# An order by hand, operation by operation, for the first stage of a memory-attention and bilinear-FFN kernel, and half of w3 w_out in three fp32r products

## The chip, the cores and the metric

The kernel runs on one core of a Trainium2 chip. The metric is the time of one execution on the device in microseconds (us), the median of the runs shown. In the text PE is the matrix engine, PEld its loading of weights, DVE the vector engine, ACT the scalar engine, SP the engine that starts the loads and stores; "granted clock" is the share of full speed that the profile records for PE.

## The reference

For each of 8 sequences (576 tokens, 8 heads of 64) an attention over 32 memories per head, then a bilinear feed-forward layer over all 4608 tokens. The weights come to the device as fp64, q, k, v and phi as fp32.

```python
a = softmax(phi, over the 32 memories)             # b h s m
k_m = einsum('bhsm,bhsd->bhmd', a, k)              # memories of keys and values
v_m = einsum('bhsm,bhsd->bhmd', a, v)
attn = softmax(q @ k_m.T / 8)                      # b h s m
x = (attn @ v_m).transpose(0, 2, 1, 3).reshape(4608, 512)
h = (x @ w1) * (x @ w2) @ w3                       # w1, w2: 512x1024, w3: 1024x1024
return h @ w_out                                   # w_out: 1024x512
```

## The kernel before

The kernel folds weights together. w3 w_out (1024x512) is made once and called W; for each sequence, v_m times w1 and w2 gives small "memory weights" (256 rows), so that x @ w1 is the softmaxed scores times them. Large products over tokens are fp32r matmuls in three parts: each operand is split into a high part (rounded to fp32r, a cast on ACT) and a low part (what is left, a subtraction on DVE, `split`, L117), and high*high, low*high and high*low are added in psum. Products that are made once, as w3 w_out, are plain fp32 matmuls.

The steps and their names in the order tables:

- Loads and conversions. `TILES` (L23 to L26) lists the weights' 26 pieces: 14 of w3's first half and w_out in turn (0 to 13), four pairs of w3's second half, w31 (14 to 17), eight of w1 and w2, w12 (18 to 25; two for each of four column groups q). They come as fp64, 512 KB for pieces 0 to 11 and 1 MB for the others. `convert` (C, L348) makes fp32 of a piece: two ACT operations on the high and low words (L370, L373), a shift on DVE (L375) and an addition on DVE (L376). `fetch` starts the loads into seven buffers, the last four pieces into the buffers of kv and q (L340).
- `product(r, k)` (W, L380): one of eight k steps of half r of w3 w_out, 4 matmuls 128x512 each (L386), into psum banks a, b, a, b (r = 0) or o, o, a, b (r = 1). `keep(r, i)` (K, L394) splits a finished bank into Wh, Wl.
- The attention of a sequence: `top`, `exp`, `norm` (softmax of phi), `turn` (transposes on PE, L187 and L191), `mem` (the memories, L202 and L211), `blocks` (transposes, L227, and km, vm on DVE), `sc` (scores, L242, and transposes on DVE, L251), `se`, `sn` (softmax), `pr` (transpose and split into ah, al).
- `N` (L295): memory weights of a column group q: 8 matmuls L301, and a split into mh, ml.
- `ab_unit` (A, L435): one of 16 units of a sequence: 12 fp32r matmuls (L447) into a and b, a copy of a on ACT, the product on DVE (gr), and its split into gh, gl.
- `out_part` (O, L463): a quarter of a 128-token block's out: 6 fp32r matmuls L471 on gh, gl, Wh, Wl.

The order: PE's and SP's instructions always stand in program order. For the first stage, `START` (L28) and the beginning of `FIRST` up to its first O, ACT's and DVE's order is given too (`by_hand`, L406), step by step: a step's instructions follow each other on each engine. After that a scheduler places ACT's and DVE's work. Sequence 0 has its 16 A units with the tail of W in between, its O parts are mixed with the attention of sequence 1, and so on (`SECOND`, `STEADY`).

## Time and profile before

| | us |
|---|---|
| median of 3 runs | 551.26 |
| lowest run, highest run | 550.85, 670.66 |
| the profiled execution | 549.36 |
| its span in the profile | 547.4 |

| engine | busy us | share of the span |
|---|---|---|
| PE | 529.7 | 97% |
| PEld | 428.1 | 78% |
| DVE | 303.5 | 55% |
| ACT | 246.0 | 45% |

Times in the profile count from the start of the span. A line of the timeline reads: start, length, engine, source line, operation, out<-in, shapes, count, and in brackets the idle time before it and what ended it. A line of the waits reads: who waited, for whom, us in total, times, longest. By the timeline the first half of w3 w_out runs from 7.8 to 37.8 us, the memories of sequence 0 follow, its second half runs from 43.3 to 73.0 us with N0 within it, the A units of sequence 0 from 74.0 to 107.1 us, its first O matmul starts at 111.39 us.

### The profile page before, as it was taken

Reading aid. Unit: us, or ns where it says so; the run is one execution under the profiler, and the core shown is the slowest. Engines: PE = TensorE matmul, PEld = TensorE weight load, DVE = VectorE, ACT = ScalarE, POOL = GpSimd, SP = SyncE. Lnnn points to the kernel's source line nnn. Section 1 sums busy time; section 2 is a strip of 40 time slices with the busy share of each in tenths; the row PEclk is TensorE's granted clock in tenths of the full one; section 3 lists DMA queues with packets and bytes.
Section 4 is the critical chain, followed back from the end, with each engine's and each line's share of the span. In section 5 each row is a group of like instructions: output and inputs, shape, how many; then the busy total and the mean of one; then the engine's idle time right before and its main releaser. Section 6 shows DMA issues by size and latency. Waiting matters only on the chain.

```text
span 547.4 us, 9722 instructions
## 1 busy us (share of the span) xinstructions
PE 529.7 (97%) x4024; PEld 428.1 (78%) x4024; DVE 303.5 (55%) x586; ACT 246.0 (45%) x502; POOL 0.7 (0%) x6
## 2 busy tenths in 40 slices
PE   4999989989999999999999999999999999999997
PEld 1443458966998689968996799869986899689985
DVE  5658886567366715593458425673567045915400
ACT  7766764635454425452544325443544044514310
POOL 0000000000000000000000000000000000000000
PEclk9999989999999999999999999999999999999999
DMA  8999436036334410072007210441021100010011
GB/s 343 420 418 418 172 114 256 1 113 230 111 147 169 173 41 21 1 279 83 20 1 281 81 40 1 155 176 50 2 74 53 40 20 2 20 45 15 1 38 57
DMA packets 14939, 64.05 MB, mean 117 GB/s; under 512 B 1712, under 2 KB 1968, under 8 KB 10032
## 3 DMA queue, kind: packets, MB, share of 16 engines
q1 hardware_dynamic: 14896, 63.45, 30.3%
q8 instruction: 31, 0.51, 0.4%
q14 instruction: 12, 0.10, 0.1%
HBM read 54.00 MB, written 9.44 MB: 116 GB/s over the span
## 4 chain that ended last, share of the span: by engine, by line
PE 91%; DVE 4%; ACT 4%; DMA 1%; issue 0%; SPq 0%; DVEq 0%; ACTq 0%
PE o L471 37%; PE a L447 19%; PE b L447 19%; PE a L386 3%; PE b L386 3%; PE a L301 2%; PE o L202 2%; PE x L301 2%; DVE w L376 1%; PE x L187 1%; PE b L301 1%; ACT w L370 1%; ACT u L373 1%; PE x L202 1%; DMA raw<-in_weights 1%; PE x L242 1%
## 5 line engine op out<-in xcount | busy, mean ns | idle before, releaser
L471 PE MATMUL o<-Wh,gh 128*128 128x512 f32 x288 | 115.1, 400 | 2.0 <-DVE Wl L119 2.0
L471 PE MATMUL o<-Wl,gh 128*128 128x512 f32 x288 | 112.9, 392 | 0.0
L471 PE MATMUL o<-Wh,gl 128*128 128x512 f32 x288 | 112.7, 391 | 0.0
L458 DVE TENSOR_TENSOR gr<-b,a_sb 128x288 f32<-128x288 f32 x128 | 58.5, 457 | 85.6 <-PE b L447 82.8
L118 ACT CAST gh<-gr 128x288 fp32r<-128x288 f32 x128 | 55.4, 433 | 103.8 <-DVE gr L458 103.8
L119 DVE TENSOR_TENSOR gl<-gr,gh 128x288 fp32r<-128x288 f32 x128 | 58.7, 459 | 63.0 <-ACT gh L118 62.9
L447 PE MATMUL a<-ah,mh 128*128 128x288 f32 x256 | 77.8, 304 | 2.2 <-ACT a_sb L456 2.2
L447 PE MATMUL a<-ah,ml 128*128 128x288 f32 x256 | 76.4, 298 | 0.0
L447 PE MATMUL b<-ah,mh 128*128 128x288 f32 x256 | 76.1, 297 | 0.0
L447 PE MATMUL b<-ah,ml 128*128 128x288 f32 x256 | 76.1, 297 | 0.0
L447 PE MATMUL a<-al,mh 128*128 128x288 f32 x256 | 75.2, 294 | 0.0
L447 PE MATMUL b<-al,mh 128*128 128x288 f32 x256 | 75.1, 293 | 0.0
L471 PEld LDWEIGHTS o<-Wh,gh 128*128 128x128 f32 x288 | 54.1, 188 | 24.8 <-issue 11.7
L489 ACT COPY osb<-o 128x512 f32<-128x512 f32 x31 | 18.1, 585 | 101.8 <-PE o L471 88.7
L471 PEld LDWEIGHTS o<-Wl,gh 128*128 128x128 f32 x288 | 54.1, 188 | 12.1
L471 PEld LDWEIGHTS o<-Wh,gl 128*128 128x128 f32 x288 | 54.2, 188 | 10.9
L447 PEld LDWEIGHTS a<-ah,mh 128*128 128x128 f32 x256 | 48.5, 189 | 5.4 <-ACT a_sb L456 2.5
L456 ACT COPY a_sb<-a 128x288 f32<-128x288 f32 x128 | 50.3, 394 | 2.0 <-PE a L447 1.7
L447 PEld LDWEIGHTS a<-al,mh 128*128 128x128 f32 x256 | 49.1, 192 | 0.3
L447 PEld LDWEIGHTS b<-al,mh 128*128 128x128 f32 x256 | 49.2, 192 | 0.0
L447 PEld LDWEIGHTS b<-ah,mh 128*128 128x128 f32 x256 | 48.6, 190 | 0.0
L447 PEld LDWEIGHTS b<-ah,ml 128*128 128x128 f32 x256 | 48.4, 189 | 0.0
(90 smaller groups left out, 633.3 us busy)
## 6 DMA issues: line engine op xcount, KB each, us to landing
kv<-in_kv SPq DMA_DIRECT2D x16, 1024.0 KB, 7.1
raw<-in_weights SPq DMA_DIRECT2D x10, 1024.0 KB, 19.4
q<-in_qT SPq DMA_DIRECT2D x8, 1152.0 KB, 10.4
out<-osb SPq DMA_DIRECT2D x31, 256.0 KB, 2.0
raw<-in_weights SPq DMA_DIRECT2D x12, 512.0 KB, 8.2
ph<-in_phiT SPq DMA_DIRECT2D x8, 576.0 KB, 3.9
kv<-in_weights SPq DMA_DIRECT2D x3, 1024.0 KB, 17.6
kv<-in_kv SPq DMA_DIRECT2D x8, 256.0 KB, 7.9
```

Source lines behind the costliest of these rows:

```text
L118: nc.scalar.copy(out=hi, in_=src)
L119: engine.tensor_tensor(out=lo, in0=src, in1=hi.bitcast(F32), op=ALU.subtract)
L187: nc.tensor.transpose(ps[:, c, t], v["ph"][:, t, at : at + P], ident)
L202: nc.tensor.matmul(ps[t][h * M : (h + 1) * M, : 2 * D], lhsT=v["a"][:, i, t, h * M : (h + 1) * M], rhs=kvt[i][:, (4 * t + h) * 2 * D : (4 ...
L242: nc.tensor.matmul(ps[t][g * M : (g + 1) * M], lhsT=km[b % 2][t * D : (t + 1) * D, g], rhs=v["q"][t * D : (t + 1) * D, g, n * HALF : (n + ...
L301: nc.tensor.matmul(ps[t][g * M : (g + 1) * M], lhsT=vm[b % 2][d, g], rhs=w12_sb[q][d, :, g], start=True, stop=True,)
L386: nc.tensor.matmul(pw[r][i], lhsT=x[:, i * P : (i + 1) * P], rhs=wos[k // half][:, k % half], start=k == 0, stop=k == NF - 1,)
L447: nc.tensor.matmul(p, lhsT=x[:, t, w, fc : fc + P], rhs=y[:, n, t * HALF : (t + 1) * HALF], start=i == 0, stop=i == len(todo) - 1,)
L456: nc.scalar.copy(out=a_sb, in_=ps[0])
L458: nc.vector.tensor_tensor(out=gr, in0=ps[1], in1=a_sb, op=ALU.mult)
L471: nc.tensor.matmul(v["p"], lhsT=x[f][:, at : at + P], rhs=y[f // half][:, f % half], start=f == 0 and k == 0, stop=f == NF - 1 and k == 2,)
L489: nc.scalar.copy(out=osb, in_=v["p"])
```

## The change

Up to the first O, the order is now a list of single operations, `START`, each word of which issues one instruction or a small group: steps are generators that stop (`yield`) after each, and a name that comes again goes on with its step. So `C5 W01 C5 C5 exp.0` puts a matmul group between the operations of one conversion. L names a load, C a conversion, W a product (one bank at a time), K a split of W, G and H a split of an operand. What stood in `FIRST` up to the first O is in `START` now, and nearly all of it stands elsewhere than before: conversions interleave with the softmax, `exp.0` is taken apart, A units overlap. The last piece's second ACT operation, as an instance, comes among the A units.

The second half of w3 w_out (r = 1) is made of high and low parts: `hi_lo` splits the four pairs of w_out (G0 to G3) and of w31 (H0 to H3), each by a cast on ACT and a subtraction on DVE of 128x1024, and `product` issues three fp32r matmuls in place of one fp32 matmul: 96 for 32. The new parts lie in buffers that are free at that time: w_out's high parts in that of w12's last column group and of al, the low parts in ah's, in w_out's own, in those of the memory weights. So w12's last group is converted late (C24, C25), after its place is free. Tags of some buffers change with that (`m_tags`, four small `wo` tiles for two large ones, W's second half in them). Loads: phi goes ahead of pieces 5 and 6, pieces 16 and 17 ahead of q.

Three places of the order. The first, on PE: the end of the memories of sequence 0 (x is the attention's psum, L202 and L211 the memories, L227 the transposes, L242 the scores, L386 the product's second half). Before:

```order
L202 MATMUL x<-kv_190,a 32x128 x8
L211 MATMUL x<-kv_192,a 32x128 x8
L227 MATMUL x<-ident,kvm 128x128 x2
L242 MATMUL x<-q,km_77 32x288 x8
L386 MATMUL o<-wo_87,w_255 128x512 x2
L386 MATMUL a<-wo_87,w_255 128x512
L386 MATMUL b<-wo_87,w_255 128x512
```

And now, where L463 is the product and woh, ah, m_299 are high and low parts of w_out and w31:

```order
L228 MATMUL x<-kv_208,a 32x128 x8
L237 MATMUL x<-kv_213,a 32x128 x8
L463 MATMUL o<-woh,m_299 128x512
L463 MATMUL o<-woh,ah 128x512
L463 MATMUL o<-ah,m_299 128x512
L463 MATMUL o<-woh,m_299 128x512
L463 MATMUL o<-woh,ah 128x512
L463 MATMUL o<-ah,m_299 128x512
L254 MATMUL x<-ident,kvm 128x128 x2
```

The transposes come after two banks of the product's first step, and the scores (not shown) 21 product matmuls later.

The second, on DVE: after km and vm of sequence 0 are there, while PE makes the product's second half. Before:

```order
L251 STREAM_TRANSPOSE s_sb<-x 128x288 x2
L258 TENSOR_REDUCE st_364<-s_sb 128x18
L259 TENSOR_TENSOR s_sb<-s_sb,st_364 128x576
L265 TENSOR_REDUCE ss_368<-s_sb 128x18
L266 TENSOR_SCALAR ss_368<-ss_368 128x18
L267 RECIPROCAL ss_368<-ss_368 128x18
L268 TENSOR_TENSOR s_sb<-s_sb,ss_368 128x576
L375 TENSOR_SCALAR w_381<-w_381 128x1024
L376 ISA w_381<-w_381,u 128x2048
```

And now, from the conversion of the last w31 pair (w_402) on:

```order
L417 ISA w_402<-w_402,u 128x2048
L447 TENSOR_TENSOR m_433<-w_374,m_417 128x1024
L447 TENSOR_TENSOR m_440<-w_402,m_435 128x1024
L280 STREAM_TRANSPOSE s_sb<-x 128x288 x2
L415 TENSOR_SCALAR w_0_81<-w_0_81 128x1024
L417 ISA w_0_81<-w_0_81,u 128x2048
L280 STREAM_TRANSPOSE s_sb<-x 128x288 x2
L287 TENSOR_REDUCE st_483<-s_sb 128x18
L289 TENSOR_TENSOR s_sb<-s_sb,st_483 128x576
```

The softmax of the scores stands behind the subtractions for w31 (L447) and among conversions of w12 (w_0 is its first column group).

The third, on PE: the memories of sequence 1. Before:

```order
L202 MATMUL x<-kv_615,a 32x128 x8
L211 MATMUL x<-kv_617,a 32x128 x8
L471 MATMUL o<-Wh_85,gh_518 128x512
L471 MATMUL o<-Wh_85,gl_526 128x512
L471 MATMUL o<-Wl_86,gh_518 128x512
```

And now:

```order
L540 MATMUL a<-ah,ml_912 128x288
L228 MATMUL x<-kv_784,a 32x128 x8
L228 MATMUL x<-kv_795,a 32x128 x8
L228 MATMUL x<-kv_784,a 32x128 x8
L228 MATMUL x<-kv_795,a 32x128 x8
L237 MATMUL x<-kv_800,a 32x128 x8
L540 MATMUL b<-ah,mh_911 128x288
```

They stood directly before the first O; they stand now within the thirteenth of the 16 A units (L540).

The diff, cut to its core (of START three lines):

```diff
 START = """
-phi0 C C C C C C C W00 C W01 C kv0 q0 top C exp W02 norm C W03 W04 C C turn4 C C W05 C turn0 W06 W07 K03 K01 K02 K00 mem blocks sc0 se0 sn0 W10 C C
-sc1 W11 C C se1 pr0 sn1 W12 W13 C C W14 C N C C C W15 W16 pr1 W17 K12
+L0 L1 L2 L3 L4 phi0 L5 C0 L6 C0 C0 L7 C0 C1 C1 C1 L8 C1 W00 W00 C2 C2 C2 W00 L9 C2 C3 C3 C3 W00 L10 C3 C4 C4 C4 W01 G0
...
+W06 C15 L21 C14 W06 C15 C15 W07 H0 C15 W07 G3 W07 H0 K01 W07 K02 K01 H1 mem.0 K02 G3 K03 K00 K03 W10 L22 mem.0 H1 L23
+C16 W10 blocks.0 K00 W10 C16 C16 W10 blocks.0 W11 C17 C16 W11 C17 W11 C17 W11 H2 C17 W12 sc1.0 H2 H3 W12 H3 W12 C18
...
 FIRST = """
-K13 N phi1 A A A kv1 A top N q1 A A A A A A N exp norm A A turn4 A A turn0 A A mem K10 K11
 O O blocks O sc0 sc1p Mp se0 q2 sn0 O O kv2 pr0 O O O se1 sn1 O Mp Mp M O pr1 O phi2 O O O O O
...
-    def split(hi, lo, src, engine=nc.vector):
+    def split(hi, lo, src):
         nc.scalar.copy(out=hi, in_=src)
-        engine.tensor_tensor(out=lo, in0=src, in1=hi.bitcast(F32), op=ALU.subtract)
+        yield
+        nc.vector.tensor_tensor(out=lo, in0=src, in1=hi.bitcast(F32), op=ALU.subtract)
...
-    m_tags = (2, 3, 4, 0, 5, 6, 7, 1)
+    m_tags = (1, 7, 2, 0, 3, 5, 4, 6)
...
-    wos = [const.tile([P, half, DO], F32, name=f"wo{i}", tag=f"wo{i}") for i in range(2)]
+    wos = [const.tile([P, 2, DO], F32, name=f"wo{i}", tag=f"wo{i}") for i in range(half)]
...
+    def hi_lo(what, k):
+        x = (wos if what == "G" else w31s)[k]
+        if what == "H":
+            hi = spare(const, f"m{k + 1}", 2 * DO)
+        elif k < 2:
+            if k == 0:
+                room = const.tile([P, 4, DO], F32R, name="woh", tag=f"w12_{NQ - 1}")
+                his["G", 1] = room[:, 2:]
+                hi = room[:, :2]
+            else:
+                hi = his["G", 1]
+        else:
+            hi = spare(att, "al", NT * S, bufs=2)
+        his[what, k] = hi
+        nc.scalar.copy(out=hi, in_=x)
+        yield
+        if k == 0:
+            lo = spare(att, "ah", NT * S, bufs=2)
+        else:
+            lo = spare(const, f"wo{k - 1}" if what == "G" else f"m{(0, 5, 6)[k - 1]}", 2 * DO)
+        los[what, k] = lo
+        nc.vector.tensor_tensor(out=lo, in0=x, in1=hi.bitcast(F32), op=ALU.subtract)
+
     def product(r, k):
...
-        x = w3s.pop((r, k))
+        x, y = w3s[r, k], wos[k // 2][:, k % 2]
+        pairs = [(x, y)]
+        if r == 1:
+            (xh, yh), (xl, yl) = [[z[what, k // 2][:, k % 2] for what in "HG"] for z in (his, los)]
+            pairs = [(xh, yh), (xl, yh), (xh, yl)]
         for i in range(4):
-            nc.tensor.matmul(
...
+            for j, (x, y) in enumerate(pairs):
+                nc.tensor.matmul(
+                    pw[r][i],
+                    lhsT=x[:, i * P : (i + 1) * P],
+                    rhs=y,
+                    start=k == 0 and j == 0,
+                    stop=k == NF - 1 and j == len(pairs) - 1,
+                )
+            yield
...
+    def go_on(what):
+        if what not in under_way:
+            under_way[what] = begin(what)
+        next(under_way[what], None)
```

## Prediction

> **What bounds the kernel now.** I read the page first, then PE's own waits, then a table by stage.

> ```profile
> span 547.4 us, 9722 instructions
> PE 529.7 (97%) x4024; PEld 428.1 (78%) x4024; DVE 303.5 (55%) x586; ACT 246.0 (45%) x502; POOL 0.7 (0%) x6
> PE 91%; DVE 4%; ACT 4%; DMA 1%; issue 0%; SPq 0%; DVEq 0%; ACTq 0%
> ```

> PE is busy 97% of the span, and 91% of the chain that ended last is PE. So the time falls only by less PE work or by shorter pauses of PE. The waits of PE, in total:

> ```profile
> PE a L386 <- DVE wo L376: 7.8, 1, 7.8
> PE a L447 <- ACT a_sb L456: 2.2, 1, 2.2
> PE o L471 <- DVE Wl L119: 2.0, 1, 2.0
> PE x L242 <- issue: 1.2, 1, 1.2
> PE x L227 <- ACT kvm L220: 0.8, 1, 0.8
> ```

> The first, 7.8 us, is the first weight on its way in; the change leaves it. The other four, 6.2 us, all lie in the first 111 us. The windows show where, and what the other engines do there (columns: window, its length, busy us of PE, PEld, DVE, ACT, POOL, granted clock, DMA share, GB/s):

> ```profile
> 7.80:37.80 30.00, 30.00 (x73) 13.54 (x73) 20.11 (x31) 22.75 (x33) 0.00 (x0) 1.00 1.02 419
> 37.80:43.30 5.50, 3.48 (x100) 2.30 (x99) 3.55 (x8) 2.68 (x6) 0.00 (x0) 1.00 1.02 419
> 43.30:74.00 30.70, 30.70 (x119) 12.46 (x112) 27.46 (x38) 24.22 (x25) 0.00 (x0) 1.00 0.65 262
> 74.00:85.60 11.60, 9.38 (x72) 8.14 (x64) 8.49 (x14) 5.30 (x12) 0.00 (x0) 0.85 0.49 184
> 96.30:111.40 15.10, 13.12 (x170) 12.43 (x162) 8.01 (x18) 9.72 (x24) 0.00 (x0) 1.00 0.01 2
> ```

> From 7.8 to 37.8 (first half of w3 w_out) PE never pauses; from 43.3 to 74 (second half) neither does it, while DVE is busy 27.46 of 30.7 us. From 74 to 85.6 there is a pause and a clock of 0.85. After 111.4 the order is the old one; I take that part over unchanged.

> **Term 1, the products.** Second half of w3 w_out: 32 fp32 matmuls go, 96 fp32r ones come. Four fp32 products, and 24 steps of an fp32r matmul of the same 128x512 shape with weights of its own each time:

> ```profile
> 51.11 1.88 PE L386 MATMUL o<-wo,w 128*128 128x512 f32 x4
> 54.54 1.88 PE L386 MATMUL o<-wo,w 128*128 128x512 f32 x4
> ...
> 118.30 0.39 PE L471 MATMUL o<-Wh,gl 128*128 128x512 f32 x1
> ...
> 123.79 0.39 PE L471 MATMUL o<-Wh,gl 128*128 128x512 f32 x1
> ```

> From 51.11 to 54.54 four products start: 3.43/4 = 0.858 us each, 27.5 us for 32. From 118.30 to 123.79 there are 24 matmuls: 5.49/24 = 0.229 us each, 22.0 us for 96. Term 1 is -5.5 us. The same shape and the same loading of weights leave little doubt here.

> **Term 2, the clock.** One stretch runs at half clock:

> ```profile
> 79.00:82.20 3.20, 3.20 (x15) 3.20 (x14) 2.20 (x5) 1.16 (x3) 0.00 (x0) 0.50 0.70 208
> 78.11 0.40 PE L447 MATMUL a<-ah,mh 128*128 128x288 f32 x1 [2.22 <-ACT a_sb L456]
> 81.01 0.44 PE L447 MATMUL a<-ah,ml 128*128 128x288 f32 x1
> 81.25 0.44 PE L447 MATMUL a<-ah,mh 128*128 128x288 f32 x1
> 87.32 0.30 PE L447 MATMUL a<-ah,mh 128*128 128x288 f32 x1
> 88.90 0.30 PE L447 MATMUL a<-ah,mh 128*128 128x288 f32 x1
> ```

> It follows the longest pause, 2.22 us. A unit of 12 matmuls takes 88.90 - 87.32 = 1.58 us, 0.132 each; in the half-clock stretch the steps are 0.24. Some 14 matmuls at 0.11 more are 1.5 us. If the change leaves no pause of that length, this goes: -1.5 us. The two other pauses, 2.0 us in all at 41 to 42.6 and 2.0 at 109 to 111, brought no slow stretch; so it may go either way near 2 us, and below 1.3 us I expect none. [...]

> **Term 3, the pauses.** First the ones that go. The 0.79 and 1.23 us stand where PE went from the memories to the transposes to the scores, each waiting for ACT or DVE to bring over what the last one made (the first place shown above). Now six product matmuls (1.4 us) stand between the memories and the transposes, and 21 more (4.8 us) ahead of the scores, so both go. In the same way the second sequence's memories come three and a half A units before the end (the third place), with their 42 matmuls behind them, and the first out matmul no longer waits 1.98 us for DVE's Wl, which is now made during the A units.

> What comes in their place is DVE's. While PE does the second half of the product, subtractions that the old order did not have stand ahead of the softmax and of the conversion of w12 (the second place). There are eight such subtractions, and eight casts on ACT. No row shows them from SBUF at 128x1024; the nearest:

> ```profile
> 76.49 0.65 DVE L119 TENSOR_TENSOR Wl<-b,Wh 128x512 fp32r<-128x512 f32 x1
> 77.07 1.21 DVE L119 TENSOR_TENSOR ml<-x,mh 128x1024 fp32r<-128x1024 f32 x1
> 60.22 0.76 DVE L119 TENSOR_TENSOR al<-at,ah 128x576 fp32r<-128x576 f32 x1 [0.74 <-ACT ah L118]
> 48.67 0.69 DVE L375 TENSOR_SCALAR w<-w 128x1024 int32<-128x1024 int32 x1
> 50.63 0.69 DVE L375 TENSOR_SCALAR w<-w 128x1024 int32<-128x1024 int32 x1
> 57.26 0.74 DVE L258 TENSOR_REDUCE st<-s_sb 128x18 f32<-128x576 f32 x1
> 18.11 1.34 DVE L165 TENSOR_REDUCE mx<-ph 128x2 f32<-128x1152 f32 x1
> 66.43 1.01 ACT L118 CAST mh<-x 128x1024 fp32r<-128x1024 f32 x1
> 31.13 1.16 ACT L370 ACTIVATE w<-raw 128x1024 f32<-128x1024 f32 x1
> ```

> For the subtraction 0.69 to 1.34 us; I take 1.21, 1.14 when the next follows at once (the 576 row, from SBUF, gives the same per column). For the cast 1.01 to 1.16; I take 1.01. A conversion's two DVE operations take 50.63 - 48.67 = 1.96 us together, a 128x512 subtraction 77.07 - 76.49 = 0.6.

> Three subtractions and three casts fall into 7.8 to 37.8: DVE 20.1 + 3.6, ACT 22.8 + 3.0 of 30 us, plus conversions that now come earlier. Before, a weight was ready 2 to 3 us ahead of its product (least 0.4, for the pair at 31 us); I walked the new order with these durations and found at least 1.4 us, so the first half keeps its pace. As for the loads, two of 1.05 MB now go ahead of q. Up to q's end the queue holds 16.7 MB:

> ```profile
> GB/s 343 420 418 418 172 114 256 1 113 230 111 147 169 173 41 21 1 279 83 20 1 281 81 40 1 155 176 50 2 74 53 40 20 2 20 45 15 1 38 57
> ```

> The first slice of 13.7 us moves 4.7 MB, the other 12.0 at 418 GB/s take 28.7 us: q is there at 42.4, 4 us before its use in the new order. The two w31 loads themselves come 2.8 us earlier.

> From 36 us, when the second w31 pair is converted, DVE has in its order, up to the low part al that the second A unit needs: 6 subtractions or low parts of 1.14, 6 of 128x512 at 0.6, 6 conversions of 1.96, some 9 us of softmax and transposes (the 0.74 row is one of them), and 2 us of small ones. This is 6.8 + 3.6 + 11.8 + 9 + 2 = 33 us: to about 70 us without a pause. PE in the same time has the memories 2.3, the product 22.0, scores and transposes 1.5 and two memory weights of 1.0: 37.8 + 27.8 = 65.6. So PE gets there first and waits on DVE. Walking all engines' orders row by row (each instruction starts when its engine is free and what it waits for is done, 0.06 us later) gives pauses at nine places between 50 and 89 us: 0.1 before the second scores, 0.8 before the first memory weight, then 0.3, 0.6, 0.6, 1.2, 0.7, 0.7 and 0.5 among the A units, 5.5 us in all, none over 1.25. The same walk of the order before gives A's start at 73.4 (trace 74.0) and pauses of 0.9, 1.25, 3.0 and 2.1 where the trace has the four above, 7.9 in all with small ones (counted from the end of a matmul's step, not of its pipeline).

> **The sum.** From the memories to the first out matmul:

> ```profile
> 37.85 1.95 PE L202 MATMUL x<-kv,a 128*32 128x128 f32 x64
> 39.73 0.45 PE L211 MATMUL x<-kv,a 64*32 64x128 f32 x16
> 46.92 0.71 PE L242 MATMUL x<-q,km 64*32 64x288 f32 x16
> 61.50 1.09 PE L301 MATMUL x<-w,vm 64*32 64x512 f32 x16
> 111.39 0.50 PE L471 MATMUL o<-Wh,gh 128*128 128x512 f32 x1 [1.98 <-DVE Wl L119]
> ```

> PE's own work between these, at full clock: the product 27.5, 16 A units of 1.58 (25.3), four memory weights of 1.0, two scores of 0.65, twice the memories (37.85 to 40.18: 2.3) and the few transposes (1.4) make 64.1 us. 73.5 us before = 64.1 + 1.5 of slow clock + 7.9 of pauses. After: 58.6 + 0 + 5.5 = 64.1, so out begins at 102.0 and everything behind it 9.4 us earlier. The profiled execution took 549.36 us (2.0 outside its span of 547.4); 538 of span then. The median shown is 551.26, so I forecast 551.26 - 9.4 = 541.9 us, a gain of 1.7%, just inside the 2% (11 us) that a measurement of this kernel can tell from no change.

> **Rivals.** (a) DVE's handovers cost more than the walk has them: PE waits for DVE from 66 on, so each of DVE's 48 operations there that is late by 0.07 us adds 3.5 us. The 27.46 of 30.7 us above speak for it, the fit of the walk to the trace before against it. Pauses of 9 us, gain 5.9: 545.4 us; with the slow stretch back, 546.9.

> (b) Slower: the clock. Between 66 and 102 us PE runs in bursts between pauses. If these keep the clock at half, every 3.2 us of it cost 1.5 us; from seven such stretches on the 9.4 are eaten and the kernel is slower, and all eleven that fit would cost 16.5: 558.4 us. For it: one pause of 2.22 did it once. Against: pauses of 0.8 and 1.2 close together did not, and none is predicted longer. [...]

> (c) The subtraction from SBUF at the low bound, 0.69: five of them inside DVE's full stretch save 2.6 us, and nearly all pauses there shrink: 2.5 left, gain 12.4: 538.9 us.

> **How the numbers follow.** Forecast 0.70, (a) 0.15, (b) 0.04, (c) 0.11. The range runs from (c), 538.9, to (a) with the slow stretch, 546.9; (b) and the edges are left out. The forecast's own spread of about 1.5 us reaches past 540.2 (2%) in a tenth of its cases, which with (c) makes faster 0.18; (b) ends inside 2%, and slower by more than that gets 0.03 for what no row here shows; the rest is 0.79.

> **What would show it.** Steps of 0.229 us in the second half of the product, and its last matmul near 65.5 us; the first A unit near 66.7, the first out matmul near 102; PE's waits after 50 us on DVE, none over 1.3 us; no stretch at 0.5 after 12 us; the 128x1024 subtraction from SBUF at 1.2 us. Wrong would be: PE waiting before 37.8 us, a pause over 2 us, or a first out matmul later than 106.

## The result and the profile after

| | before | after |
|---|---|---|
| median of 6 runs each | 550.86 | 540.92 |
| lowest run | 549.45 | 539.76 |
| the profiled execution | 549.36 | 540.96 |
| its span | 547.4 | 539.0 |

The ratio is 0.9818, 95% interval 0.9803 to 0.9833; 541.9 us was forecast. One of the six runs of before took 670.66 us, in a slow state, and the ratio leaves it out. A second measurement of the changed kernel, beside the run with the later maximum (below), gave 540.29 us and 0.983 (0.9817 to 0.9844).

The head of the page after, with the share of the engines in the chain that ended last, and the granted clock in 40 slices of 13.5 us:

```profile
span 539.0 us, 9799 instructions
PE 525.2 (97%) x4056; PEld 432.8 (80%) x4056; DVE 310.1 (58%) x594; ACT 252.8 (47%) x510; POOL 0.7 (0%) x6
PEclk9999999999999999999999999999999999999999
```

PE is as full as before, at 97%, but its busy time is 4.5 us less, with 32 records more (96 of the new products for 64: an fp32 product has two). PE's waits after:

```profile
PE a L463 <- DVE wo L417: 7.4, 1, 7.4
PE b L540 <- DVE gr L553: 1.7, 2, 1.5
PE x L335 <- DVE w L417: 0.7, 2, 0.4
PE x L209 <- DVE ml L132: 0.2, 1, 0.2
```

Behind the first weight 2.6 us are left of 6.2, all on DVE. None of the four places of before is among them. By stage (columns as before: window, length, busy us of PE, PEld, DVE, ACT, POOL, clock, DMA share, GB/s):

```profile
7.80:37.80 30.00, 30.00 (x71) 13.45 (x71) 24.04 (x35) 27.96 (x40) 0.00 (x0) 1.00 1.02 419
40.20:65.50 25.30, 25.07 (x180) 18.07 (x173) 24.33 (x36) 21.47 (x24) 0.00 (x0) 1.00 0.88 358
65.50:80.00 14.50, 12.72 (x94) 10.60 (x93) 13.36 (x23) 11.77 (x24) 0.00 (x0) 1.00 0.18 67
...
89.50:102.00 12.50, 12.38 (x163) 10.78 (x163) 7.30 (x16) 5.97 (x15) 0.00 (x0) 1.00 0.23 95
```

The first half of the product has no pause. In the second half DVE is busy 24.33 of 25.30 us and PE 25.07: both are full. PE pauses mostly between 65.5 and 80. The clock is 1.00 in all four stages shown. The marks of the stages on PE's timeline: the memories, two steps inside the second half of the product, its last matmul, the first A unit, the first out matmul:

```profile
38.87 1.95 PE L228 MATMUL x<-kv,a 128*32 128x128 f32 x64
...
44.25 0.39 PE L463 MATMUL o<-woh,m 128*128 128x512 f32 x1
...
46.34 0.40 PE L463 MATMUL b<-woh,m 128*128 128x512 f32 x1
...
66.69 0.40 PE L463 MATMUL b<-wo,m 128*128 128x512 f32 x1
...
68.04 0.41 PE L540 MATMUL a<-ah,mh 128*128 128x288 f32 x1
...
103.11 0.39 PE L566 MATMUL o<-Wh,gh 128*128 128x512 f32 x1
```

From 44.25 to 46.34 there are nine steps: 0.232 us each. Set beside before and the forecast, stage by stage:

| from, to | before | forecast | after |
|---|---|---|---|
| start of the span, memories | 37.85 | 37.85 | 38.87 |
| memories, first A unit | 36.2 | 28.9 | 29.17 |
| first A unit, first out matmul | 37.4 | 35.3 | 35.07 |
| first out matmul, end of the span | 436.0 | 436.0 | 435.9 |

So the time came from where it was forecast, 9.3 us between the memories and the first out matmul against 9.4; the profiled execution gained only 8.4 because its first 38.87 us were 1.0 longer. That one is the clock's start. The first products, after and then before:

```profile
7.38 2.08 PE L463 MATMUL a<-wo,w 128*128 128x512 f32 x2 [7.38 <-DVE wo L417]
9.25 1.91 PE L463 MATMUL b<-wo,w 128*128 128x512 f32 x2
...
13.76 1.02 PE L463 MATMUL a<-wo,w 128*128 128x512 f32 x2
```

```profile
7.80 2.08 PE L386 MATMUL a<-wo,w 128*128 128x512 f32 x2 [7.80 <-DVE wo L376]
...
11.02 1.02 PE L386 MATMUL a<-wo,w 128*128 128x512 f32 x2
```

One product takes 1.7 to 1.9 us from start to start until the clock is granted in full, and 0.86 behind that. (The clock column does not tell: it reads 1.00 from the start of the span, since the profile's record of the clock begins with that moment.) That came at 13.13 us in this execution of the changed kernel and at 10.65 in that of before, where the two records begin. It is no property of the change: in the profile of the kernel with four subtractions on POOL (below), whose PE order up to there is the same, the full clock comes by the steps of its products at 10.9 and the memories start at 37.76; in the one with the later maximum at 12.4 and 38.49. At 1.71 us a product in place of 0.86, half of each us of slow clock is lost.

### The profile page after: what moved, and what is told of

It is laid out like the page before. It is cut to its first block, busy times and chain, and to the rows that moved or that the text cites. A ratio compares the mean times of both kernels' runs of the same rounds, so it can differ in the third digit from the quotient of the medians.

```text
span 539.0 us, 9799 instructions
## 1 busy us (share of the span) xinstructions
PE 525.2 (97%) x4056; PEld 432.8 (80%) x4056; DVE 310.1 (58%) x594; ACT 252.8 (47%) x510; POOL 0.7 (0%) x6
## 4 chain that ended last, share of the span: by engine, by line
PE 92%; DVE 5%; DMA 1%; ACT 1%; issue 1%; DVEq 0%; ACTq 0%
PE o L566 37%; PE a L540 18%; PE b L540 18%; PE a L463 3%; PE b L463 3%; PE a L335 2%; PE o L228 2%; PE x L335 2%; DVE w L417 1%; PE x L209 1%; PE b L335 1%; PE x L228 1%; DMA ph<-in_phiT 1%; PE o L463 1%; PE x L270 1%
## 5 line engine op out<-in xcount | busy, mean ns | idle before, releaser
L566 PE MATMUL o<-W,gh 128*128 128x512 f32 x288 | 96.7, 396 | 0.0
L540 PE MATMUL b<-ah,mh 128*128 128x288 f32 x256 | 75.5, 295 | 1.7 <-DVE gr L553 1.7
L540 PE MATMUL a<-ah,mh 128*128 128x288 f32 x256 | 77.0, 301 | 0.1
L540 PE MATMUL b<-al,mh 128*128 128x288 f32 x256 | 75.5, 295 | 0.0
L540 PE MATMUL a<-ah,ml 128*128 128x288 f32 x256 | 75.5, 295 | 0.0
L540 PE MATMUL a<-al,mh 128*128 128x288 f32 x256 | 75.5, 295 | 0.0
L540 PE MATMUL b<-ah,ml 128*128 128x288 f32 x256 | 75.4, 294 | 0.0
L566 PEld LDWEIGHTS o<-W,gh 128*128 128x128 f32 x288 | 54.1, 188 | 17.3 <-issue 5.9
L566 PE MATMUL o<-Wh,gh 128*128 128x512 f32 x144 | 57.1, 397 | 0.0
L566 PE MATMUL o<-Wh,gl 128*128 128x512 f32 x144 | 56.4, 392 | 0.0
L566 PE MATMUL o<-Wl,gh 128*128 128x512 f32 x144 | 56.4, 392 | 0.0
L566 PE MATMUL o<-W,gl 128*128 128x512 f32 x144 | 56.4, 391 | 0.0
L540 PEld LDWEIGHTS a<-ah,mh 128*128 128x128 f32 x256 | 48.1, 188 | 3.3 <-issue 1.0
L540 PEld LDWEIGHTS b<-ah,mh 128*128 128x128 f32 x256 | 48.1, 188 | 2.4 <-DVE gr L553 2.2
L540 PEld LDWEIGHTS a<-al,mh 128*128 128x128 f32 x256 | 48.2, 188 | 0.3
L540 PEld LDWEIGHTS b<-ah,ml 128*128 128x128 f32 x256 | 48.1, 188 | 0.0
L540 PEld LDWEIGHTS a<-ah,ml 128*128 128x128 f32 x256 | 48.1, 188 | 0.0
```

Of the source, the lines that this page charges most:

```text
L540: nc.tensor.matmul(p, lhsT=x[:, t, w, fc : fc + P], rhs=y[:, n, t * HALF : (t + 1) * HALF], start=i == 0, stop=i == len(todo) - 1,)
L566: nc.tensor.matmul(v["p"], lhsT=x[f][:, at : at + P], rhs=y[f], start=f == 0 and k == 0, stop=f == NF - 1 and k == 2,)
```

## The experiments

All ratios are to the kernel before, measured beside it on the same chip. The experiments ran on several chips, so a difference of two medians from different experiments is less sure than the ratios.

**The order alone.** The new order, but the second half of the product stays fp32, and the splits G and H go.

```diff
-        if r == 1:
+        if False:
...
-L0 L1 L2 L3 L4 phi0 L5 C0 L6 C0 C0 L7 C0 C1 C1 C1 L8 C1 W00 W00 C2 C2 C2 W00 L9 C2 C3 C3 C3 W00 L10 C3 C4 C4 C4 W01 G0
+L0 L1 L2 L3 L4 phi0 L5 C0 L6 C0 C0 L7 C0 C1 C1 C1 L8 C1 W00 W00 C2 C2 C2 W00 L9 C2 C3 C3 C3 W00 L10 C3 C4 C4 C4 W01
```

> The changed order, but the second half of w3 w_out again as 32 fp32 matmuls, without the eight casts and subtractions. Theory (the products give 5.5 us, the order the rest): the product takes 27.5 us again instead of 22.2, DVE's pauses in the A units stay, so some 5 to 7 us above the changed kernel: 545 to 548 us, ratio to before about 0.99 to 0.995. Rival (DVE alone paces that stretch, PE's saving is lost in waits): within 2 us of the changed kernel, 541 to 543.

Measured: 548.51 us, 0.9967 (0.995 to 0.9983). No stretch at half clock (the mean granted clock of the profile is 1.000), and these waits of PE:

```profile
PE x L334 <- DVE ml L131: 1.4, 1, 1.4
PE b L539 <- DVE gr L552: 1.1, 2, 0.6
PE a L539 <- DVE al L131: 1.0, 2, 0.7
...
```

With three of 0.2 to 0.4 us that are not shown these are 4.4 us of pauses, smaller and at new places, against 6.2 before. So the order takes away the slow stretch and the long pauses, and by itself gains 0.3%; the products in this order are worth another 7.6 us by the medians (548.51 to 540.92) and 8.0 by the profiles (from the memories to the first out matmul 72.2 to 64.2), a little more than the 5 to 7 expected. Some 5 of these are PE's own work and 1.8 the pauses (4.4 to 2.6); the rest was not traced, nor why the fp32 variant has more pauses.

**The products alone.** The three fp32r products with their splits, but every step given whole, in the manner of the order before (a step's instructions follow each other). The first half of the scores' last step, pr0, had to stand later, since its buffer holds a part of w_out.

```diff
-C16 W10 blocks.0 K00 W10 C16 C16 W10 blocks.0 W11 C17 C16 W11 C17 W11 C17 W11 H2 C17 W12 sc1.0 H2 H3 W12 H3 W12 C18
+blocks.0 sc0.0 sc0.0 se0.0 se0.0 se0.0 sn0.0 sn0.0 sn0.0 W10 W10 W10 W10 C16 C16 C16 C16 L23 C17 C17 C17 C17 L24 sc1.0
```

> The products in three fp32r parts with the eight splits, but whole steps one after the other as in the kernel before (probs of sequence 0 later, since its buffers hold high and low parts). Theory (the casts and subtractions stand in the queues of ACT and DVE and only the fine order hides them): pauses of PE of 2 to 3.6 us at the memories, the scores, the memory weights and the first A units, some 20 us in all; slower than before by 2 to 10 us, 553 to 561, and more than one stretch at half clock. Rival (the products give their 5.5 us by themselves, the order adds the rest): 545 to 546 us.

Measured: 560.46 us, 1.0173 (1.0131 to 1.0214). Slower than before. PE's waits, and the two stretches at half clock:

```profile
PE x L269 <- issue: 2.8, 1, 2.8
PE a L539 <- ACT a_sb L549: 2.7, 2, 2.1
PE x L253 <- ACT kvm L246: 2.3, 1, 2.3
PE a L539 <- ACT ah L129: 2.3, 1, 2.3
PE o L565 <- DVE W L131: 2.0, 1, 2.0
...
```

```profile
46.60:53.20 6.60, 4.72 (x24) 3.06 (x25) 4.28 (x10) 0.88 (x2) 0.00 (x0) 0.50 1.02 426
80.70:94.20 13.50, 10.49 (x39) 9.48 (x40) 10.09 (x15) 8.61 (x14) 0.00 (x0) 0.50 0.22 80
```

The splits stand as whole steps ahead of everything behind them, PE waits 2 us and more at five places, and 20.1 us run at half clock. The control has whole steps in the same way, but fp32 products and no splits:

> The control for the products alone: fp32 products, whole steps one after the other in the changed program's words. If its order is that of the kernel before in what matters, 550 to 552 us; by the walk of its order it is 4.8 us slower than the kernel before, 554 to 556, since the last splits of W and probs stand otherwise. With it the products alone cost (560.5 minus this). Theory: 4 to 7 us dearer at whole steps, and no half-clock stretch longer than 3.4 us here. Rival (the products alone save their 5.5 us): this would have to be 566.

Measured: 558.47 us, 1.0166 (1.0132 to 1.0199), with runs from 555.4 to 561.0 and a mean granted clock of 0.994 in its profile, which is some 6.6 us at half clock. So whole steps in the changed program's words are already slower than the kernel before by 1.7%, and the products bring nothing there (560.46 against 558.47, intervals that overlap), neither the 4 to 7 us of loss that were expected nor a saving, while in the new order they bring some 8 us. The profiles show where PE's saving goes: with the products PE's waits behind the first weight are 15.6 us and half clock lasts 20.1, without them (in a run of 555.4 us) 10.1 and some 6.6. The two halves of the change do not add up: of the orders tried, the products pay where the order hides their splits.

**The memories of sequence 1 last.** Only mem.1 and the splits K10 and K11 go back to the end, directly before the first out.

```diff
-turn4.1 A10 A11 mem.1 A11 A12 A12 mem.1 A13 A12 A12 A13 A13 A12 A14 A13 A13 A14 A14 A13 A15 A14 A14 A15 A15 A14 A15
+C25 A8 A9 C25 A9 A9 N3 A9 A8 A9 A8 A9 A8 A10 N3 A10 A10 N3 A11 A10 A11 A11 A10 turn4.1 A12 A11 turn4.1 A10 A11 A11 A12
+A12 A13 A12 A12 A13 A13 A12 A14 A13 A13 A14 A14 A13 A15 A14 A14 A15 A15 A14 A15 A15 A15 mem.1 mem.1 K10 K10 K11 K11
```

> The changed kernel, but the memories of sequence 1 and the splits of the first two banks of W's second half (K10, K11) stand directly before the first out matmul, as before. Theory: DVE's Wl is late again, a pause of 2 us before the first out matmul, 543 us. Rival (that pause is hidden by something else that waits there anyway): 541 us.

Measured: 542.0 us, 0.9856 (0.9819 to 0.9892). The pause of before is back in full, at the same place, and no half clock behind it (mean granted clock 1.000):

```profile
PE o L565 <- DVE W L131: 2.0, 1, 2.0
...
```

The medians differ by 1.1 us, within the intervals; in the profile the stretch from the memories to the first out matmul is 66.0 us (38.07 to 104.09) in place of 64.2 and 64.8 in the two profiles of the changed kernel, so 1.2 to 1.8 us there are this move's. The wait is for the split of W, so it may be K10 and K11 that count and not the memories; they were not moved apart.

**Four subtractions on POOL.** G3, H1, H2 and H3, all in DVE's full stretch, move to another engine.

```diff
-        nc.vector.tensor_tensor(out=lo, in0=x, in1=hi.bitcast(F32), op=ALU.subtract)
+        engine = nc.gpsimd if (what, k) in (("G", 3), ("H", 1), ("H", 2), ("H", 3)) else nc.vector
+        engine.tensor_tensor(out=lo, in0=x, in1=hi.bitcast(F32), op=ALU.subtract)
```

> The changed kernel, with four of the eight subtractions (G3, H1, H2, H3) on POOL instead of DVE. As the prediction has it (33 us of DVE work in a row set the start of the A units), 4.6 us less work on DVE takes 2 to 4 us of pauses away: 537 to 539 us. Rival (the chain of softmax, conversion and buffers in the order sets it, not the amount of work): at most 0.7 us, 540 to 541 us. A POOL subtraction of more than 4 us would make it slower.

Measured: 541.65 us, 0.9839 (0.9811 to 0.9867): no gain. Rows of POOL, and DVE's idle places in the same stretch (in brackets):

```profile
36.52 2.69 POOL L448 TENSOR_TENSOR wo<-wo,al 128x1024 fp32r<-128x1024 f32 x1 [35.22 <-ACT al L440]
...
46.04 5.76 POOL L448 TENSOR_TENSOR m<-w,m 128x1024 fp32r<-128x1024 f32 x2 [4.47 <-ACT m L440]
```

```profile
39.06 0.69 DVE L132 TENSOR_TENSOR Wl<-b,Wh 128x512 fp32r<-128x512 f32 x1 [0.74 <-ACT Wh L130]
...
41.88 0.69 DVE L415 TENSOR_SCALAR w<-w 128x1024 int32<-128x1024 int32 x1 [1.52 <-ACT w L407]
...
47.52 0.85 DVE L280 STREAM_TRANSPOSE s_sb<-x 128x288 f32<-128x288 f32 x2 [0.84 <-PE x L270]
...
49.88 3.00 DVE L417 CUSTOM_DVE_ANT_0 w<-w,u 128x2048 uint16<-128x2048 uint16 x1 [0.35 <-ACT u L413]
52.80 0.83 DVE L280 STREAM_TRANSPOSE s_sb<-x 128x288 f32<-128x288 f32 x2
```

DVE got rid of four operations of 1.22, 4.9 us. It spent most of them waiting for ACT and for the scores (0.74, 1.52, 0.84, 0.47 and 0.35 us), and one conversion takes 3.00 us in place of 1.22. The last two rows in the changed kernel:

```profile
51.74 1.22 DVE L417 CUSTOM_DVE_ANT_0 w<-w,u 128x2048 uint16<-128x2048 uint16 x1
52.88 0.84 DVE L280 STREAM_TRANSPOSE s_sb<-x 128x288 f32<-128x288 f32 x2
```

So DVE came to this conversion 1.9 us earlier than in the changed kernel (PE to the memories 1.1), and left it level, at 52.80 against 52.88. From there to the first A unit DVE has no idle time over 0.15 us in either profile, and that unit starts at 67.96, against 68.04. PE's wait for the first weight of w12 grew from 0.23 to 1.3 us. The run therefore does not settle whether less DVE work would bring the A units forward: most of what it gave went into other waits, and the stretched conversion took the rest. Behind DVE's queue stands ACT's, busy 21.47 of 25.30 us in the changed kernel.

**The scores first.** The rest of the memories, the transposes and the first scores stand ahead of the product again.

```diff
-W06 C15 L21 C14 W06 C15 C15 W07 H0 C15 W07 G3 W07 H0 K01 W07 K02 K01 H1 mem.0 K02 G3 K03 K00 K03 W10 L22 mem.0 H1 L23
-C16 W10 blocks.0 K00 W10 C16 C16 W10 blocks.0 W11 C17 C16 W11 C17 W11 C17 W11 H2 C17 W12 sc1.0 H2 H3 W12 H3 W12 C18
+W06 C15 L21 C14 W06 C15 C15 W07 H0 C15 W07 G3 W07 H0 K01 W07 K02 K01 H1 mem.0 K02 G3 K03 K00 K03 mem.0 blocks.0
+blocks.0 sc1.0 W10 L22 H1 L23 C16 W10 K00 W10 C16 C16 W10 W11 C17 C16 W11 C17 W11 C17 W11 H2 C17 W12 H2 H3 W12 H3 W12
```

> The changed kernel, but the transposes (blocks) and the first scores of sequence 0 stand ahead of the second half of w3 w_out on PE again, as before. Theory (PE had waited there for ACT and DVE, and the product in between covers it): pauses of 0.8 and 1 to 2 us return near 41 to 43 us, part is given back because a later pause before the first memory weight (0.2) goes; 2 us more than the changed kernel, 542 to 543.5. Rival (PE only waits for DVE later in its place): 541 us.

Measured: 545.74 us, 0.9921 (0.9902 to 0.994), dearer than either theory had it. The two waits:

```profile
41.82 0.44 PE L254 MATMUL x<-ident,kvm 128*128 128x128 f32 x2 [0.79 <-ACT kvm L247]
...
44.98 1.21 PE L270 MATMUL x<-q,km 64*32 64x288 f32 x16 [2.72 <-DMA q<-in_qT]
```

q lands only just before 44.98; it now stands behind two more weights in the queue. At least 6.7 us at half clock follow it (0.50 from 43.6 to 50.3), and a later pause has at least another 3.2 behind it (0.50 from 84.6 to 87.8). So the 27 product matmuls in front of the scores cover not only DVE's and ACT's handover but the load of q, which the change itself made later.

**The maximum later.** In the changed kernel the longest pause, 1.54 us, is at 77.77, ahead of the second half (b) of the fifth A unit, which waits for the product gr of the third. What DVE does ahead of it:

```profile
75.63 1.35 DVE L186 TENSOR_REDUCE mx<-ph 128x2 f32<-128x1152 f32 x1 [1.04 <-DMA ph<-in_phiT]
76.90 0.45 DVE L132 TENSOR_TENSOR gl<-gr,gh 128x288 fp32r<-128x288 f32 x1
77.27 0.45 DVE L553 TENSOR_TENSOR gr<-b,a_sb 128x288 f32<-128x288 f32 x1
```

It stands 1.04 us at the maximum of sequence 1's phi until that is loaded (the load starts at 71.19, when the last split of the softmax has freed the buffer), then takes 1.35 us for it, and only then makes that gr, which frees the bank that PE waits for. The edit moves that one word:

```diff
-N1 C22 A1 A0 K11 A1 N1 A1 A0 A2 A1 A0 A2 A1 top.1 A2 A3 A3 A1 A3 A2 exp.1 C23 A4 A2 exp.1 A4 A3 A2 A4 A5 C22 A3 C24 A5
+N1 C22 A1 A0 K11 A1 N1 A1 A0 A2 A1 A0 A2 A1 A2 A3 A3 A1 A3 A2 top.1 exp.1 C23 A4 A2 exp.1 A4 A3 A2 A4 A5 C22 A3 C24 A5
```

> The changed kernel with one word moved: the maximum over phi of sequence 1 (top.1 on DVE) stands three DVE operations later, behind the product gr of the third A unit. Theory (DVE stood 1.0 us at that maximum until phi had landed, and PE's pause of 1.54 us waits for the gr behind it): the pause falls below 1.1 us, 0.3 to 1 us less than the changed kernel in the same call. Rival (what is behind on DVE is as late anyway): no difference.

Beside it on the same chip the changed kernel once more:

> The changed kernel once more, as the yardstick for the two others of this call: 540.5 to 541.5 us.

Measured: 539.9 us, 0.9825 (0.9811 to 0.9838), and for the changed kernel 540.29, 0.983 (0.9817 to 0.9844). The longest pause for a gr, in the one (now ahead of b of the sixth unit; at the fifth there is none over 0.15 us) and the other (at the fifth):

```profile
77.98 0.40 PE L540 MATMUL b<-ah,mh 128*128 128x288 f32 x1 [0.55 <-DVE gr L553]
```

```profile
78.16 0.40 PE L540 MATMUL b<-ah,mh 128*128 128x288 f32 x1 [2.16 <-DVE gr L553]
```

The cause of the pause is shown: 2.16 us (1.54 in the first profile) go from the fifth unit, and 0.55 come at the sixth. As a time the 0.4 us are within the intervals. From the memories to the first out matmul it is 63.7 us, against 64.2 and 64.8 in the two profiles of the changed kernel.

**Whole orders, tuned.** Three orders found by moving many words at a time from the second half of the product to the middle of the A units. In all three some of the scores' transposes (pr) stand ahead of the last normalization (sn), so a part of the scores is used without the division by its sum; the instructions are the same. These three do not compute the reference, and their times show only what an order can do. (A first such order, which read a bank of W before its sum was complete, has no time.)

```diff
-pr0.0 W17 sn1.0 W17 pr0.0 sn1.0 C24 W17 pr0.0 W17 sn1.0 K12 N1 pr1.0 K13 K10 K12 pr1.0 K13 C25 A0 pr1.0 A0 C23 phi1 A0
+pr0.0 C23 W17 sn1.0 sn1.0 W17 W17 K12 W17 K10 N1 sn1.0 pr1.0 pr0.0 K12 pr1.0 phi1 K13 C24 A0 pr1.0 A0 C23 C25 A0 K13
```

> The changed kernel with some twenty words of the order moved, so that the maximum of sequence 1, the second softmax and the conversions of w12's third group stand later on DVE and the first products gr earlier; by a walk of the orders with the rows' durations PE's pauses among the A units are 1.1 us smaller: 539 to 540 us, ratio to before 0.981 or below (the changed kernel 0.983, the one with the maximum moved 0.9825). Rival (pauses this small are within the walk's error): 0.983.

> Another such order, pauses among the A units 1.3 us smaller by the walk, but 1.4 us before the first memory weight: 539 to 540 us, ratio 0.981. Rival: 0.983.

> A third such order, with the last splits of W behind the first A unit: 1.6 us less by the walk, with one pause of 1.7 us at the first A units that may fall into one clock window: 538.5 to 540 us, ratio 0.980. Rival: 0.983, or slower by 1.5 us if that pause brings a stretch at half clock.

Measured: 539.0 us, 0.9798 (0.9775 to 0.9821); 540.0, 0.9814 (0.9791 to 0.9837); 538.9, 0.9795 (0.9771 to 0.9818). To see whether the gain of the third came from what it left undone, its order was mended: the last sn0 ahead of its transpose, the load of phi behind the last split, the end of K13 ahead of the first unit.

```diff
-C20 sn0.0 C21 N0 C20 C21 W15 C21 N0 W15 W15 C22 W15 C22 se1.0 W16 sn0.0 se1.0 W16 C23 L25 W16 se1.0 pr0.0 N0 W16 sn0.0
-pr0.0 C23 W17 sn1.0 sn1.0 W17 W17 K12 W17 K10 N1 sn1.0 pr1.0 pr0.0 K12 pr1.0 phi1 K13 C24 A0 pr1.0 A0 C23 C25 A0 K13
+C20 sn0.0 C21 N0 C20 C21 W15 C21 N0 W15 W15 C22 W15 C22 se1.0 W16 sn0.0 se1.0 W16 C23 L25 W16 sn0.0 pr0.0 N0 W16 se1.0
+pr0.0 C23 W17 sn1.0 sn1.0 W17 W17 K12 W17 K10 N1 sn1.0 pr1.0 pr0.0 K12 pr1.0 K13 C24 K13 A0 pr1.0 A0 phi1 C23 C25 A0
```

> The order of the third of the three tuned runs, with three words moved back so that every value is read after it is made: the last normalization of the first half of the scores ahead of its transpose, the load of the second phi behind the last split, the second half of W's split ahead of the first unit. Same instructions as the changed kernel, about as many words moved as in the tuned runs. Theory (the changed kernel's remaining pauses are a matter of order alone): memories to first out matmul 62.9 to 63.4 us against 64.2 in the changed kernel, PE waits of at most 1.8 us after 8 us, time 538.8 to 539.6 us, ratio 0.979 to 0.981. Rival (what the tuned runs gained came from the reads that did not wait): PE waits of 2.2 us or more, 63.7 us or more from memories to first out matmul, 539.9 to 540.6 us, as the run with the later maximum.

Measured: 539.23 us, 0.9793 (0.9774 to 0.9811). PE's waits behind the first weight:

```profile
PE a L539 <- DVE al L131: 0.9, 1, 0.9
PE b L539 <- DVE W L131: 0.6, 1, 0.6
PE x L334 <- DVE w L416: 0.2, 1, 0.2
PE a L539 <- ACT a_sb L549: 0.2, 1, 0.2
```

1.9 us of waits in place of 2.6, and 63.1 us from the memories to the first out matmul (37.60 to 100.67). The first A unit starts at 66.76, 29.2 us behind the memories as in the changed kernel; what is gained lies behind it (33.9 us in place of 35.1). So order alone is worth about 1 us more than the changed kernel has: this is the fastest kernel here that leaves nothing out, by the ratios 0.25 to 0.4% ahead of the changed kernel; its interval overlaps that of the changed kernel's first measurement and stays clear of the second's.

## Why the prediction held, point by point

The time forecast was 541.9 us, the median 540.92; the other way round, the profiled execution was to be 540.0 and took 540.96. Each matmul counted from its start to the start of PE's next instruction, and what exceeds the step put down as a pause, the stretch from the memories to the first out matmul adds up as follows:

| us | forecast | after |
|---|---|---|
| 96 product matmuls | 22.0 | 23.0 |
| 16 A units at 0.132 a step | 25.3 | 25.3 |
| memory weights, scores, memories, transposes | 11.3 | 10.9 |
| pauses and changes of shape among the product and the A units | 5.5 | 4.9 |
| sum | 64.1 | 64.2 |

That the sums agree to 0.1 us is in part luck: the products cost 1.0 us more than forecast, the pauses 0.6 and the small matmuls 0.4 less.

- **Term 1, the products: -5.5 forecast, -5.0 measured.** The step is 0.232 us in a row, not 0.229, and where a product matmul follows one of another shape it takes 0.32 to 0.34: eight such places behind scores, transposes and memory weights cost 0.8 us. The row the price came from was an unbroken run. In the same count the fp32 products of before took 28.1, not 27.5.
- **Term 2, the clock: -1.5, right.** No stretch at half speed behind the start: the record of the clock is full from 13.13 to 538.78 us, the last 0.2 of the span aside. But the reason given, "below 1.3 us pause I expect none", was too simple, and the margin thin: in the second profile of the changed kernel the pause was 2.16 us, as long as the one of before that did it, and it went without (below).
- **Term 3, the pauses: 7.9 to 5.5 forecast, to 4.9 measured.** The three places named are free, and the third came back when the memories and the splits K10 and K11 did (the run with the memories last). At the first the reason named was half of it: the run with the scores first waited 2.72 us there for q. The load itself came 2.5 us later than forecast, near 44.9 and not at 42.4.
- **"PE gets there first and waits on DVE": right, but for the longest pause.** The waits are DVE's, and between 36 and 69 us DVE has no idle time over 0.15 us at any place in the changed kernel, as the 33 us "without a pause" had it; the first A unit starts 29.2 us behind the memories, 28.9 forecast. The longest pause, 1.2 us by the forecast and 1.5 and 2.2 measured, is not of that sum: a maximum in DVE's order waits for a load there, and moving one word took most of the pause. That the sum of DVE's work sets the first A unit is not shown. Four subtractions less did not move it, but in that run most of the relief went into waits for ACT and for the scores, and a conversion stretched by 1.8 us took the rest.
- **The signs of being wrong.** PE did not wait before 37.8 us, and the first out matmul at 103.11 was not later than 106. "A pause over 2 us" did come, in the second profile, without the loss of time that it was to tell of.
- **The first half keeps its pace: right**, 30.00 of 30.00 us. It ended 1.0 us late from the clock's start, which the sum did not hold: in the prediction it was taken as fixed at before's.
- **The subtraction from SBUF: 1.21 forecast, 1.22 measured**, so rival (c) fell. (The 576-column row named beside it gives 1.35 by columns, 0.76 x 1024/576, not the same as 1.21.) Two that follow at once take 2.55, against 1.14 + 1.21 = 2.35:

```profile
14.92 1.22 DVE L447 TENSOR_TENSOR ah<-wo,woh 128x1024 fp32r<-128x1024 f32 x1
...
47.72 2.55 DVE L447 TENSOR_TENSOR m<-w,m 128x1024 fp32r<-128x1024 f32 x2
```

- **Rival (a)**, dearer handovers, did not come: 4.9 us of pauses, not 9. **Rival (b)**, the clock, did not come either, but it is no empty threat: the products in whole steps had it for 20 us and were slower than before.

## What to carry to other kernels

Three fp32r products of split operands cost PE less than one fp32 product (0.70 against 0.86 us here), but the splits come due on DVE and ACT at one time: with whole steps they brought nothing, with an order that puts single operations between the matmuls some 8 us. Price the matmuls from a run of the trace with the same changes of shape around them, and look in the other engines' orders for an instruction that waits for a load ahead of one that PE needs; its place, not the engine's sum of work, made the longest pause here.

## What the runs showed of the hardware

```profile
75.50:78.90 3.40, 1.18 (x9) 0.94 (x9) 3.40 (x6) 1.46 (x3) 0.00 (x0) 1.00 0.00 0
```

```profile
40.10:43.50 3.40, 1.37 (x39) 0.67 (x30) 2.07 (x7) 2.71 (x5) 0.00 (x0) 1.00 1.01 415
```

```profile
74.20:77.60 3.40, 1.80 (x14) 1.57 (x12) 1.75 (x3) 1.06 (x4) 0.00 (x0) 1.00 0.03 9
77.60:81.00 3.40, 2.64 (x18) 2.41 (x18) 3.40 (x6) 3.40 (x8) 0.00 (x0) 1.00 0.00 0
```

Six windows at full clock with PE busy 0.44 to 1.54 us of 3.40 had half clock behind them: the two above with 1.18 and 1.37, 1.54 and 1.44 in the control with whole steps (from 41.3 and 78.8 us; its mean clock of 0.994 is that of two steps at half), 0.44 and 1.09 with the products alone (from 43.2 and 77.3, by PE's timeline). Those with 1.80 (above) and 1.86 (the first profile of the changed kernel, from 74.6) had none. Between them, with 1.61 the next window stayed at full clock (before, from 109.6 us), with 1.64 it did not (scores first, from 81.1 us); the windows are laid to 0.1 us, so these two do not differ. The pause of 2.16 us, which the edge at 77.6 cuts, had full clock behind it, the one of 2.22 inside a window half clock that cost some 1.5 us. In the six windows PE was idle for 1.86 us or more, over half of the step. How long a stretch lasts was not settled.

**DVE and POOL.** The conversion that took 3.00 us started at 49.88, during a POOL subtraction that ended at 51.80, and ended 1.08 us behind it: about its own length, as if it had stood until then. This is one row; what held the conversion is not shown. A subtraction of 128x1024 takes 2.4 to 2.9 us on POOL and 1.22 on DVE.
